# Holding four loads behind the first weight quarter, two 256-column pieces to a PSUM bank, and two later chunk pairs

## The chip, the cores and the metric

The program runs on one core of one Trainium2 chip. The metric is the device time of one execution in microseconds; the figure given for a kernel is the median of several executions. A profile is one further execution, recorded by the hardware profiler. Its span runs from the first to the last instruction of the core and is a little shorter than that execution's device time.

The engines have the profile's names: PE (matrix multiplies, with PEld for its weight loads), DVE, ACT, POOL and SP. SP issues most loads, POOL issues the weight loads and most stores, and both kinds of transfer are carried by the core's 16 DMA engines.

## The reference

A retention layer (a linear recurrence per head) feeds a low-rank mixer with a two-layer MLP.

```python
def _attn_ref(q, k, v):                      # B=4, H=8, S=768, D=64
    gamma = 1.0 - 2.0 ** (-5.0 - np.arange(H))
    for t in range(S):
        state = gamma * state + np.einsum('bhd,bhe->bhde', k[:, :, t], v[:, :, t])
        y[:, :, t] = scale * np.einsum('bhd,bhde->bhe', q[:, :, t], state)

def _moe_ref(x, U, V, w_ch1, w_ch2):         # x: 4 x 768 x 512, rank 32, hidden 2048
    xt = x.transpose(0, 2, 1)
    h = xt @ U @ V
    u = x + h.transpose(0, 2, 1)
    ch = np.maximum(u @ w_ch1, 0.0) @ w_ch2
    return u + ch
```

All inputs and the output are float32.

## The kernel before

The four batches go one after the other. The sequence of 768 positions is cut into six chunks of 128, handled as three pairs (chunks 0 and 1, 2 and 3, 4 and 5). Batch 0's attention is written out by hand as the string `STEPS` and runs first, while the weights are loaded. From there on PE's order is made by `weave` (the last lines of the body): the MLP of batch b is a list of pieces with costs in microseconds of PE time (41.472 in all for a batch), and the attention of batch b+1, with the rest of the low-rank product, is a list of marks. A mark is placed at a fraction of the list's cost, and it is emitted before the first piece that begins at or behind that fraction. Every engine executes its instructions in the order in which they are emitted.

**The MLP of a batch** (`mlp_pieces`). There are 16 hidden blocks `m` of 128 rows. `up(m, 0, 512)` makes four matmuls of 512 columns into one PSUM bank, and a relu evicts the bank to `gT`; this is done for all 16 blocks. Then `up(m, 512, 256)` does the same for the remaining 256 columns, 16 times, each with a bank and a relu of its own. Every third relu goes to DVE (L427), the others to ACT (L429). Last come 24 pieces of `down` (L445), four to each of six row blocks `j`; the fourth evicts through DVE (L452). PSUM banks with the tag `mlp` are three in number and are shared by `up`, `down` and, for batch 1, the PE transposes of k and q (`turn_k1` L257, `turn_q1` L271) and `lr_proj_turn`. A new bank waits for the eviction of what it held.

**The attention of batches 1 to 3.** For a chunk `ci`: `prep` scales or casts k, q and v (POOL or ACT, L81, L83, L77) into buffers of which there are four for each of the three; `turn_*` transposes k and q; `score` (L281) makes the scores of one chunk in the PSUM tile `R[ci % 2]` and DVE masks them (L284); `mix` writes the chunk's result over the same tile (L297, L302), ACT evicts it to `x` (L70), PE updates the state (L313), and ACT evicts the state to `nsz` in two instructions. In the table `AT`, batch 1 has the entries `(0.565, 0.095, (0.045, 0.09), (0.075, 0.045), None)`: the first pair's score stands at 0.565, each later pair's 0.095 behind it, the mixes 0.045 and 0.09 behind their score, and the transposes of k and q 0.075 and 0.045 before it. The ACT casts of k are marked at 0.51 (chunks 2 and 3) and 0.63 (chunks 4 and 5). `lr_proj_turn` stands at 0.875 and `lr_uT`, which makes the MLP's input of batch 1, at 0.915.

**The loads around the weights.** w1 comes in four quarters of 512 columns and w2 in four parts, all issued by POOL in one queue and cast on the way. Step `w0` issues w1's first quarter behind a POOL copy that waits for batch 0's last q load, and `w1` the second. The first MLP matmuls of batch 0 (`begin_up`, L400) need the first quarter. Loads of batches 1 to 3 are issued by SP in the fixed order `feed` through a ring of 20 buffers; `feed_more` issues as many as `n_open` and the ring allow. Behind `STEPS`, six loads of batch 1 are let go at once (k, q and v of chunks 0 and 1). The rest stand behind a gate: POOL copies one element of w1's column 1023 into the next ring buffer, so that the load into this buffer, and every load queued behind it on SP, waits until the second quarter has landed.

Of the kernel before, what the change touches and what calls it, by code (L numbers as in the profile page):

```python
# [16 lines left out]
def kernel(  # L17
# [11 lines left out]
    nc = tc.nc  # L29
# [98 lines left out]
    def feed_more(t=None):  # L128
        while n_fed[0] < n_open[0] and n_held[0] < RING:
            nm, b, ci = key = feed[n_fed[0]]  # L130
            n_fed[0] += 1
            n_held[0] += 1
            ready[key] = t = ring() if t is None else t
            if (nm, b) == ("q", 1):
                load_heads(t, q, 1, ci % 2, ci // 2)
            else:
                nc.sync.dma_start(
                    out=t.rearrange("p (h d) -> p h d", h=H),
                    in_=src_of[nm][b, :, ts(ci, P), :].rearrange("h p d -> p h d"))
            t = None  # L140
# [269 lines left out]
    def mlp_pieces(b):  # L410
        gT = gtp.tile([P, NM, S], bf16, tag="gT", name=f"gT_{b}")
        pieces = []
        n = [0]

        def up(m, lo, sz):
            def f():
                g_p = begun.pop((b, m, lo), None)
                c0 = 3 if g_p is not None else 0
                if not c0:
                    g_p = bank("mlp")  # L420
                for c in range(c0, NCB):
                    nc.tensor.matmul(g_p[:, :sz], w1b[:, c, ts(m, P)],  # L422
                                     uTs[b][:, c, ds(lo, sz)], start=(c == 0),
                                     stop=(c == NCB - 1))
                n[0] += 1
                if n[0] % 3 == 0:
                    nc.vector.tensor_relu(gT[:, m, ds(lo, sz)], g_p[:, :sz])  # L427
                else:
                    nc.scalar.activation(gT[:, m, ds(lo, sz)], g_p[:, :sz],  # L429
                                         AF.Relu)  # L430
            return f

        for m in range(NM):
            pieces.append((0.864, up(m, 0, LO)))
        for m in range(NM):
            pieces.append((0.432, up(m, LO, S - LO)))
        hold = {}

        def down(j, m0, n0=0, nn=DM):
            def f():  # L440
                if m0 == 0:
                    hold[j, n0] = bank("mlp")
                ch = hold[j, n0]
                for m in range(m0, m0 + 4):
                    nc.tensor.matmul(ch[:, :nn], gT[:, m, ts(j, P)],  # L445
                                     w2b[:, m, ds(n0, nn)],
                                     start=(m == 0), stop=(m == NM - 1))
                if m0 == NM - 4:
                    o_sb = outp.tile([P, DM], fp32, tag="o_sb",
                                     name=f"o_{b}_{j}_{n0}")[:, :nn]  # L450
                    n = ds(n0, nn)
                    nc.vector.tensor_tensor(o_sb, ch[:, :nn], us[b][:, j, n],  # L452
                                            op=ALU.add)
                    if n0:
                        nc.sync.dma_start(out=out[b, ts(j, P), n], in_=o_sb)
                    else:
                        stores.append((nc.gpsimd, out[b, ts(j, P), n], o_sb))
            return f

        for j in range(NCK):  # L460
            if (b, j) == (B - 1, NCK - 1):
                for n0, nn in ((0, 384), (384, 128)):
                    for m0 in range(0, NM, 4):
                        pieces.append((0.864 * nn / DM, down(j, m0, n0, nn)))
                continue
            for m0 in range(0, NM, 4):
                pieces.append((0.864, down(j, m0)))
        return pieces
# [204 lines left out]
    def step(s):  # L673
        if s[0] == "F":
            s, n = s[1:].split(":")
            return fill(s[:-1], int(s[-1]), int(n))
        if s == "Va":
            return nc.gpsimd.tensor_copy(out=V1b, in_=V1)
        if s == "Vb":
            for i, n in enumerate((512, 256)):  # L680
                nc.tensor.matmul(R[1][:, i, :n], rep4, V1b[:, ds(512 * i, n)],
                                 start=True, stop=True)
            return
        if s == "Vc":
            return evac("D", V4, R[1].rearrange("p i n -> p (i n)")[:, :S])
        nm, at = s.rstrip("0123456789."), s.lstrip("KQVWTkqSmsMNxtPpcERUbuwB")
        u = int(at[0]) if at else 0
        eng = BY[nm][u] if nm in BY and nm != "pc" else None
        if nm in ("K", "Q", "V"):
            if eng == "S":  # L690
                cast_unit("v", u, "P", 0, 2)
            else:
                cast_unit(nm.lower(), u, eng)
        elif nm == "W":
            cast_unit("v", u, "D", 2, 2)
        elif nm in ("Tk", "Tq"):
            turn_unit(nm[1], u)
        elif nm in ("kT", "qT"):
            turned_unit(nm[0], u, eng)
        elif nm == "S":  # L700
            score_unit(u)
        elif nm == "m":
            mask_unit(u)
        elif nm == "ST":
            state_unit(u, int(at[2]))
        elif nm == "s":
            state_out(u, int(at[2]), eng)
        elif nm == "M":
            mix_unit(u)
        elif nm == "N":  # L710
            query_unit(u, False)
        elif nm == "x":
            x_out(u, eng)
        elif nm == "Ub":
            evac("A", Ub, Uf)
        elif nm == "xt":
            x_turn(u)
        elif nm == "P":
            proj(u, range(NCK if u == 0 else 4))
        elif nm == "R":  # L720
            proj(1, range(4, NCK))
        elif nm == "pc":
            pc_out(u // 2, BY["pc"][u // 2])
        elif nm == "E":
            expand((0, 1) if u == 0 else (u,))
        elif nm == "B":
            for m in range(2):
                begin_up(m, (0, 1) if u == 1 else (2,))
        elif nm == "u":
            evac(eng, uTs[0][:, u, :LO], xT[u][:, :LO])  # L730
        elif nm == "w":
            if u == 0:
                nc.gpsimd.tensor_copy(out=gate0, in_=ready["q", 5][:1, :1])
            load_w1(512 * u, 512)
        else:
            raise ValueError(s)
# [9 lines left out]
    pieces0 = mlp_pieces(0)  # L746
    for s in STEPS.split():
        step(s)
    n_open[0] = 6
    feed_more()  # L750
    n_open[0] = 6 * NCK
    for mb in range(2, 4):
        load_w1(512 * mb, 512)
    for j in range(4):
        load_w2(j)
    gate = ring()
    nc.gpsimd.tensor_copy(out=gate[:1, :1], in_=w1b[:1, NCB - 1, 1023:1024])
    feed_more(gate)
    for t in nsz:
        nc.gpsimd.memset(t, 0.0)  # L760
    for nm in "kqv":
# [1 line left out]

    AT = {1: (0.565, 0.095, (0.045, 0.09), (0.075, 0.045), None),
          2: (0.255, 0.17, (0.05, 0.095), (0.175, 0.11),
              (0.0, 0.085, 0.17, 0.255, 0.34, 0.425)),
          3: (0.20, 0.20, (0.05, 0.095), (0.19, 0.145),
# [11 lines left out]
    for b in range(1, B):  # L781
        s0, step, dm, dt, at_prep = AT[b]
        for ci in range(NCK):
            pair_at = b - 1 + s0 + step * (ci // 2)
            if b == 1:
                mark(pair_at - dt[0], turn_k1, ci)
                mark(pair_at - dt[1], turn_q1, ci)
            else:
                mark(b - 1 + at_prep[ci], prep_chunk, b, ci)
                mark(pair_at - dt[ci % 2], turn_chunk, b, ci)  # L790
            mark(pair_at, score, b, ci)
            mark(pair_at + dm[ci % 2], mix, b, ci)
            if b > 2:
                mark(b - 2 + 0.25 + 0.1 * ci, open_chunk)
        if b == 1:
            for nm, eng, at in (("k", "A", (0.51, 0.63)), ("q", "P", (0.54, 0.66)),
                                ("v", "P", (0.58, 0.70))):
                for pp in (1, 2):
                    mark(at[pp - 1], prep_two, nm, pp, eng)
            mark(0.875, lr_open, b)  # L800
            mark(0.875, lr_proj_turn, b)
            mark(0.915, lr_uT, b)
            mark(1.11, lr_expand, b, 0, 4)
        else:
            l0, l1, l2, l3 = LR
            mark(b - 1 + l0, mixed, b)
            mark(b - 1 + l1, lr_expand, b, 0, 4)
            mark(b - 1 + l2, lr_turn, b, 0)
            mark(b - 1 + l3, lr_turn, b, 2)
        mark(b + 0.02, lr_expand, b, 4, 2)  # L810
        mark(b + 0.08, lr_turn, b, 4)
# [35 lines left out]
```

## Time and profile before

| What | Value |
|---|---|
| Device time, 3 runs | 228.85, 228.23 and 228.86 us; median 228.85 us |
| Device time of the profiled execution | 227.64 us |
| Its span, first to last instruction | 225.8 us |
| Granted PE clock in the span | 1.000 |
| DVE busy | 98.7 us (44%) |
| ACT busy | 86.7 us (38%) |
| POOL busy | 78.5 us (35%) |
| HBM read, written | 27.46 MB, 6.29 MB |

Busy time is the union of an engine's recorded instructions. Matmuls overlap and their ends are modelled, so a short wait of PE shows in the distance between starts before it shows as idle time. A row of the timeline gives the start, the length, the engine, the line, the tiles (out<-in), the shapes and how many equal instructions were merged; in square brackets stands the idle time before it and what ended it.

### The profile page before, as it was taken

Reading aid. Unit: us, or ns where it says so; the run is one execution under the profiler, and the core shown is the slowest. Engines: PE = TensorE matmul, PEld = TensorE weight load, DVE = VectorE, ACT = ScalarE, POOL = GpSimd, SP = SyncE. Lnnn points to the kernel's source line nnn. Section 1 sums busy time; section 2 is a strip of 40 time slices with the busy share of each in tenths; the row PEclk is TensorE's granted clock in tenths of the full one; section 3 lists DMA queues with packets and bytes.
Section 4 is the critical chain, followed back from the end, with each engine's and each line's share of the span. In section 5 each row is a group of like instructions: output and inputs, shape, how many; then the busy total and the mean of one; then the engine's idle time right before and its main releaser. Section 6 shows DMA issues by size and latency. Waiting matters only on the chain.

```text
span 225.8 us, 4802 instructions
## 1 busy us (share of the span) xinstructions
PE 216.5 (96%) x1982; PEld 122.8 (54%) x1982; DVE 98.7 (44%) x148; ACT 86.7 (38%) x180; POOL 78.5 (35%) x112
## 2 busy tenths in 40 slices
PE   7999899999899999999999999999999999999991
PEld 2567344875565544588454444686554444764451
DVE  6578536346734346625426145361624242312111
ACT  3776354554653134575230044746030044530000
POOL 5588581108720069380100496710101100001010
PEclk9999999999999999999999999999999999999999
DMA  5999999999999995889994554411113330001211
GB/s 164 336 290 249 219 198 197 196 244 221 281 253 238 247 276 98 187 186 187 206 269 133 163 139 90 99 26 25 46 49 120 115 93 0 0 3 48 93 77 64
DMA packets 89303, 34.59 MB, mean 153 GB/s; under 512 B 71217, under 2 KB 87729, under 8 KB 89281
## 3 DMA queue, kind: packets, MB, share of 16 engines
q1 hardware_dynamic: 83152, 23.86, 47.4%
q0 software_dynamic: 6128, 10.42, 18.2%
q8 instruction: 15, 0.25, 0.4%
q14 instruction: 8, 0.06, 0.1%
HBM read 27.46 MB, written 6.29 MB: 149 GB/s over the span
## 4 chain that ended last, share of the span: by engine, by line
PE 49%; issue 32%; DMA 5%; SPq 5%; POOL 4%; ACT 1%; DVE 1%; POOLq 0%
PE mlp L422 23%; PE mlp L445 18%; SPq L106 5%; DMA w1b<-in_moe_w_ch_dram 3%; POOL out_dram L408 3%; DMA in<-in_q_dram 2%; PE r L281 1%; PE r L302 1%; POOL vd L83 1%; PE r L297 1%; PE st L313 1%; PE r L344 1%; PE mlp L400 1%; DVE a L284 1%; PE mlp L271 1%
## 5 line engine op out<-in xcount | busy, mean ns | idle before, releaser
L445 PE MATMUL mlp<-w2b,gT 128*128 128x512 bf16 (+2 forms) x400 | 87.8, 371 | 0.0
L422 PE MATMUL mlp<-uT,w1b 128*128 128x512 bf16 (+1 forms) x506 | 86.4, 325 | 0.5 <-ACT gT L429 0.4
L429 ACT ACTIVATE gT<-mlp 128x512 bf16<-128x512 f32 (+1 forms) x88 | 42.3, 490 | 70.5 <-PE mlp L422 69.5
L422 PEld LDWEIGHTS <-w1b 128*128 128x128 bf16 x506 | 48.3, 98 | 32.5 <-issue 1.4
L445 PEld LDWEIGHTS <-gT 128*128 128x128 bf16 x400 | 37.0, 98 | 39.2 <-issue 0.2
L408 POOL DMA_DIRECT2D out_dram<-o x24 | 13.3, 553 | 109.1 <-DVE o L452 105.7
L427 DVE TENSOR_SCALAR gT<-mlp 128x512 bf16<-128x512 f32 (+1 forms) x40 | 22.1, 556 | 41.3 <-PE mlp L422 41.2
L452 DVE TENSOR_TENSOR o<-mlp,u 128x512 f32<-128x512 f32 (+2 forms) x25 | 16.7, 670 | 51.0 <-PE mlp L445 50.8
L284 DVE TENSOR_TENSOR a<-r,mask 128x1024 bf16<-128x1024 f32 x18 | 21.3, 1219 | 5.2 <-PE r L281 3.8
L83 POOL TENSOR_TENSOR vd<-in,gk 128x512 bf16<-128x512 f32 x18 | 18.6, 1040 | 10.0 <-PE mlp L422 5.7
L70 ACT ACTIVATE x<-r 128x512 bf16<-128x512 f32 x20 | 11.9, 596 | 25.1 <-PE r L302 24.0
L351 DVE TENSOR_TENSOR u<-r,x 128x512 bf16<-128x512 f32 (+1 forms) x16 | 14.5, 950 | 4.2 <-PE r L344 4.2
L83 POOL TENSOR_TENSOR qd<-in,gq 128x512 bf16<-128x512 f32 x12 | 12.5, 1039 | 0.0
L70 ACT ACTIVATE nsz<-st 64x256 bf16<-64x256 f32 x30 | 11.1, 372 | 0.3
L81 POOL CAST kd<-in 128x512 bf16<-128x512 f32 x14 | 8.5, 608 | 6.8 <-issue 6.2
L83 POOL TENSOR_TENSOR qp<-in,gq 128x512 bf16<-128x512 f32 x6 | 6.1, 1040 | 7.5 <-DMA in<-in_q_dram 6.0
L578 DVE TENSOR_TENSOR a<-r,mask 128x1024 bf16<-128x1024 f32 x6 | 7.3, 1220 | 2.1 <-PE r L571 2.1
L302 PE MATMUL r<-vd,a 128*128 128x64 bf16 x144 | 7.1, 193 | 0.0
L281 PE MATMUL r<-qT,kT 64*128 64x128 bf16 x144 | 5.8, 217 | 0.9 <-ACT x L70 0.9
L302 PEld LDWEIGHTS <-a 128*128 128x128 bf16 x144 | 6.0, 98 | 0.7
L281 PEld LDWEIGHTS <-kT 64*128 64x128 bf16 x144 | 4.1, 94 | 4.1 <-issue 4.0
L297 PEld LDWEIGHTS <-qT 128*128 128x128 bf16 x60 | 4.6, 98 | 2.7
(108 smaller groups left out, 143.2 us busy)
## 6 DMA issues: line engine op xcount, KB each, us to landing
in<-in_k_dram SPq DMA_DIRECT2D x24, 256.0 KB, 4.7
in<-in_q_dram SPq DMA_DIRECT2D x24, 256.0 KB, 4.8
in<-in_v_dram SPq DMA_DIRECT2D x24, 256.0 KB, 5.0
out_dram<-o POOLq DMA_DIRECT2D x23, 256.0 KB, 2.4
w1b<-in_moe_w_ch_dram POOLq DMA_DIRECT2D x4, 512.0 KB, 10.5
w2b<-in_moe_w_ch_dram POOLq DMA_DIRECT2D x4, 512.0 KB, 20.5
kT<-kd SPq DMA_TRANSPOSE x12, 2.4
qT<-qd SPq DMA_TRANSPOSE x12, 2.4
```

Source lines behind the costliest of these rows:

```text
L70: nc.scalar.activation(dst, src, AF.Copy)
L83: e.tensor_tensor(dst, src, scale, op=ALU.mult)
L281: nc.tensor.matmul(r[:, i, ts(hp, P)], kT[ri, hp], qT[ri, hp], start=True, stop=True)
L284: nc.vector.tensor_tensor(a, r.rearrange("p i (n m) -> p i n m", n=4), mask[:, None, None, :].to_broadcast([P, 2, 4, P]), op=ALU.mult)
L302: nc.tensor.matmul(o[:, ts(h, D)], a[:, i, hp], vb[:, h], start=(ci == 0 and h == 0), stop=True, skip_group_check=True)
L351: nc.vector.tensor_tensor(v4(us[b][:, ds(j0, nj), e]), R[g][:, :, :nj * P].rearrange("p c (j e) -> p c j e", j=nj), v4(xs[b][:, ds(j0, nj) ...
L408: eng.dma_start(out=dst, in_=src)
L422: nc.tensor.matmul(g_p[:, :sz], w1b[:, c, ts(m, P)], uTs[b][:, c, ds(lo, sz)], start=(c == 0), stop=(c == NCB - 1))
L427: nc.vector.tensor_relu(gT[:, m, ds(lo, sz)], g_p[:, :sz])
L429: nc.scalar.activation(gT[:, m, ds(lo, sz)], g_p[:, :sz], AF.Relu)
L445: nc.tensor.matmul(ch[:, :nn], gT[:, m, ts(j, P)], w2b[:, m, ds(n0, nn)], start=(m == 0), stop=(m == NM - 1))
L452: nc.vector.tensor_tensor(o_sb, ch[:, :nn], us[b][:, j, n], op=ALU.add)
```

## The change

Three things change.

1. The six loads are split. The two k loads go at once; the four loads of q and v stand behind a new gate on w1's column 511 (the last of its first quarter). On POOL, the third quarter of w1 is issued before this gate, the fourth quarter and w2 behind it. The gate on column 1023 stays for the rest of the loads.
2. The 16 pieces of 256 columns become eight pieces of two blocks. Each writes both halves of one bank with eight matmuls, and one relu evicts both. `relu` is now a helper that still gives every third eviction to DVE, so a batch has 24 instead of 32 relus.
3. Batch 1's score marks become 0.565, 0.685 and 0.80 (before: 0.565, 0.66 and 0.755). The mixes and transposes of k and q move with their pair; the casts of `prep_two` stay. `lr_open` and `lr_proj_turn` move from 0.875 to 0.905 and `lr_uT` from 0.915 to 0.94.

```diff
+        def relu(dst, src):
+            n[0] += 1
+            if n[0] % 3 == 0:
+                nc.vector.tensor_relu(dst, src)
+            else:
+                nc.scalar.activation(dst, src, AF.Relu)
+
...
-        for m in range(NM):
-            pieces.append((0.432, up(m, LO, S - LO)))
+        def up_two(m):
+            def f():
+                g_p = bank("mlp")
+                for n in range(2):
+                    for c in range(NCB):
+                        nc.tensor.matmul(g_p[:, ts(n, S - LO)], w1b[:, c, ts(m + n, P)],
+                                         uTs[b][:, c, LO:], start=(c == 0),
+                                         stop=(c == NCB - 1))
+                relu(gT[:, ds(m, 2), LO:], g_p.rearrange("p (n t) -> p n t", n=2))
+            return f
+
+        for m in range(0, NM, 2):
+            pieces.append((0.864, up_two(m)))
...
+    def feed_behind(col):
+        gate = ring()
+        nc.gpsimd.tensor_copy(out=gate[:1, :1], in_=w1b[:1, NCB - 1, col:col + 1])
+        feed_more(gate)
+
+    n_open[0] = 2
+    feed_more()
+    load_w1(1024, 512)
     n_open[0] = 6
-    feed_more()
+    feed_behind(511)
     n_open[0] = 6 * NCK
-    for mb in range(2, 4):
-        load_w1(512 * mb, 512)
+    load_w1(1536, 512)
     for j in range(4):
         load_w2(j)
-    gate = ring()
-    nc.gpsimd.tensor_copy(out=gate[:1, :1], in_=w1b[:1, NCB - 1, 1023:1024])
-    feed_more(gate)
+    feed_behind(1023)
...
-    AT = {1: (0.565, 0.095, (0.045, 0.09), (0.075, 0.045), None),
+    AT = {1: ((0.565, 0.685, 0.80), None, (0.045, 0.09), (0.075, 0.045), None),
...
-            pair_at = b - 1 + s0 + step * (ci // 2)
+            pair_at = b - 1 + (s0[ci // 2] if b == 1 else s0 + step * (ci // 2))
...
-            mark(0.875, lr_open, b)
-            mark(0.875, lr_proj_turn, b)
-            mark(0.915, lr_uT, b)
+            mark(0.905, lr_open, b)
+            mark(0.905, lr_proj_turn, b)
+            mark(0.94, lr_uT, b)
```

More of the change, by code (lines that the diff above doesn't have):

```diff
@@ L424, in f @@
                                      stop=(c == NCB - 1))
[L425 to L430, printed above, removed]
+                relu(gT[:, m, ds(lo, sz)], g_p[:, :sz])
             return f
```

## The prediction

> **What bounds the kernel now.** The first view is the page's head, the second PE's waits (microseconds in total, times, longest).
>
> ```profile
> span 225.8 us, 4802 instructions
> PE 216.5 (96%) x1982; PEld 122.8 (54%) x1982; DVE 98.7 (44%) x148; ACT 86.7 (38%) x180; POOL 78.5 (35%) x112
> ```
> ```profile
> PE r L281 <- ACT x L70: 0.9, 1, 0.9
> PE mlp L400 <- DMA w1b<-in_moe_w_ch_dram: 0.7, 1, 0.7
> PE mlp L422 <- ACT gT L429: 0.4, 2, 0.2
> ```
>
> PE sets the end. No matmul is removed, so only PE's waits can be won, and three are named here: a score behind ACT, the first MLP matmul behind w1, `up` behind relus. The third is larger than it looks, since matmul ends are modelled; the timeline's starts tell it. First batch 3 without attention (60 matmuls of 512 columns and 64 of 256 in one row), then the 256-column stage of batch 1, then that of batch 2.
>
> ```profile
> 180.31 20.11 PE L422 MATMUL mlp<-uT,w1b 128*128 128x512 bf16 x124
> 200.26 20.92 PE L445 MATMUL mlp<-w2b,gT 128*128 128x512 bf16 x112
> ```
> ```profile
> 97.71 1.47 PE L422 MATMUL mlp<-uT,w1b 128*128 128x256 bf16 x12
> 99.41 1.91 PE L422 MATMUL mlp<-uT,w1b 128*128 128x256 bf16 x16 [0.23 <-ACT gT L429]
> 101.25 0.62 PE L281 MATMUL r<-qT,kT 64*128 64x128 bf16 x16
> 101.80 2.55 PE L422 MATMUL mlp<-uT,w1b 128*128 128x256 bf16 x20
> 104.19 0.39 PE L297 MATMUL r<-nsz,qT 128*128 128x128 bf16 x4
> ...
> 104.87 1.04 PE L422 MATMUL mlp<-uT,w1b 128*128 128x256 bf16 x8
> 105.74 1.03 PE L445 MATMUL mlp<-w2b,gT 128*128 128x512 bf16 x4
> ```
> ```profile
> 145.01 4.25 PE L422 MATMUL mlp<-uT,w1b 128*128 128x512 bf16 x32
> ...
> 155.62 2.75 PE L445 MATMUL mlp<-w2b,gT 128*128 128x512 bf16 x12
> ```
>
> Batch 3: 60 matmuls of 512 columns and 64 of 256 take 19.95, so 0.217 and 0.1084 each: the price without waits. Batch 1, 97.71 to 105.74: 8.03, less 56 x 0.1084 = 6.07, the score (0.55) and the mix (104.19 to 104.87, 0.68), leaves 0.73. Batch 2, 145.01 to 155.62: 10.61, less 4 x 0.217, 64 x 0.1084, 0.55 and 2 x 0.68, leaves 0.89. About 0.1 each is PE's switch into a score (0.31 between starts instead of 0.217, also where nothing waits). Waits: 0.63 + 0.79 = 1.42.
>
> **The w1 quarter.** Transfers on the two queues (packets, MB, share of 16 engines) from 21 to 23 us:
>
> ```profile
> q0 software_dynamic: 374, 0.38, 118.0%
> q1 hardware_dynamic: 36, 0.01, 2.5%
> ```
> From 23 to 24 us:
> ```profile
> q1 hardware_dynamic: 389, 0.20, 69.2%
> q0 software_dynamic: 76, 0.07, 52.7%
> ```
> From 27 to 47 us:
> ```profile
> q0 software_dynamic: 3105, 3.08, 90.6%
> q1 hardware_dynamic: 3102, 0.84, 30.3%
> ```
>
> q0 is the weights', with 1 KB a packet, so a quarter is 512. Alone it moves 187 a us; from 23 the batch 1 loads share, and it moves 76. By 23 it has moved 84 (20 to 21) + 374; the 54 left end near 23.8 now, near 23.3 alone. The quarter lands at 25.48 (17.99 + 7.49 in the chain) and PE starts at 25.52. I move the landing 0.5 to 0.7 earlier; PE is ready at 24.83, DVE's casts of uT follow until 26.14 and cap it. Gain 0.6 (bounds 0 and 0.70, the whole wait).
>
> What is moved: POOL's gate holds w1's last quarter and w2's four issues, before at 22.0 to 25.8, to about 24.9 to 28.9. Quarters two and three stay queued (landed 29.1 and 32.6, some 7 us of work), so q0 does not run dry, at no cost. Behind the gate on POOL also stand the second gate, the memsets of `nsz` and the casts of chunks 0 and 1, which PE first wants at 47.55. On SP the four loads, and all behind them, start some 6.5 later than 17.9. They are 2 x 512 packets (512 B) and 2 x 1,024 (256 B); with the weights they go one for one, 155 a us each (3,105 in 20 us), and alone 785 (5,101 in 49.5 to 56). The next, k of chunk 3, is the one that PE comes to wait for: it landed at about 50.5, where ACT's cast of it began; qT behind the cast ended at 51.78, the score came at 52.18. Before this k stand the same weight and load packets as now, and the DMA row of the page shows 9 in every slice from 6 to 84 us, so it still lands near 50.5. The score is wanted 0.3 earlier (0.6 here less 0.28 below) with 0.4 of cover; I take 0.1 of loss (bounds 0 and 0.4). Every us beyond costs one. v's two POOL casts are wanted by the mixes at 54.9 and 58.1, and at a landing of 44.2 + 6.5 they are still in time.
>
> **Two pieces to a bank.** ACT's relu is 0.38 for 256 columns and 0.60 for 512, DVE's 0.42 and 0.69. What makes PE wait is ACT's queue: an `x` (0.60) and two `nsz` (0.77) stand before a relu, while the three banks cover 3 x 0.432 = 1.30 of PE. With 3 x 0.864 = 2.59 they cover it, as in the 512-column pieces with the same marks (92.55 to 97), where PE keeps its pace. I walked the built order of batches 1 and 2 with these durations: the least room is 0.3, behind DVE's two masks (2.4). Gain 1.42 (bounds: a loss of 0.22 ACT or 0.27 DVE at each of the two named waits, 0.5, and 1.42). One loss is certain: batch 0's first `down` takes the bank of the last relu, now eviction 24 on DVE. It waited until 48.18 behind 0.41 on ACT from 47.72; 0.69 makes it 0.28 later.
>
> The Trainium skill, "Perfetto Trace Analysis", section "Optimizing Scalar/DVE Operations", speaks against this edit: engines that are not saturated but cause bubbles elsewhere should get smaller instructions. ACT at 38% and DVE at 44% are such engines. By the rule the two named waits grow by 0.5 in all instead of 1.42 going, and the total is +0.4, about 229.2. I go by the rows, as the bank rotation doubles with the instruction.
>
> **The later pairs.** ACT and PE around the long wait:
>
> ```profile
> 58.28 0.39 PE L313 MATMUL st<-vd,kd 128*128 128x128 bf16 x4
> ...
> 58.76 0.63 ACT L77 ACTIVATE kd<-in 128x512 bf16<-128x512 f32 x1 [0.91 <-issue]
> ...
> 59.29 0.58 ACT L70 ACTIVATE x<-r 128x512 bf16<-128x512 f32 x1
> ```
>
> The k cast of chunk 5 needs chunk 1's buffer, which its state matmuls free at 58.67; `x` of chunk 1 stands behind the cast, and the score of chunk 3 behind `x`: 1.08 lost. Before it, a q transpose waits 0.29 for a bank (55.37 to 55.88). The set-back puts four down matmuls (0.87) between mix and score. But the cast stays at 0.63, and in the built order the eviction of qT of chunk 2 (0.74) now stands behind it, and kT of chunk 2 (0.60) behind `x` and `nsz` of chunk 0. Counted from chunk 0's mix V: `nsz` ends at V+1.70, kT at V+2.32, so the q transpose, ready at V+1.80, waits 0.57. Chunk 1's state ends near V+4.5; cast, qT and `x` end at V+5.24, 5.88 and 6.32; the two scores, ready at V+5.31 and 6.13, wait 0.6 and 0.25. That is 1.44 for 1.37: cost 0.07 (bounds: all 1.37 won, 0.6 lost if the next bank waits too). `lr_uT` loses two `down` pieces of cover: DVE's eviction of R[1] (1.21) ends 1.66 after its matmuls start, PE has 2.1 of work: 0.
>
> **Sum.** -0.60 (w1) - 1.42 (relus) + 0.28 (last eviction) + 0.07 (pairs) + 0.05 (uT's cast) + 0.10 (k of chunk 3) = -1.52. Span 225.8 to 224.3; the profiled execution 227.64 to 226.1. The median of the runs is 1.2 above that execution: 228.85 - 1.52 = 227.3.
>
> **Rivals.**
> - The set-back works in full: the pairs' 1.44 goes too, 227.3 - 1.44 = 225.9. For: the score's wait is the largest named. Against: the order on ACT.
> - The waits only move: relus hold banks 0.2 longer and the quarter is late (0.2 won), so -0.2 + 0.5 + 0.28 + 0.07 = +0.65 at worst, and with half of the bank gain -0.2 - 0.7 + 0.35 = -0.55; the middle is 228.9. For: only 0.3 of room behind the masks.
> - Slower: the held loads are late for chunk 3's k cast. If the 6.5 of later start came through in full, k would land at 57.0; at half, 53.75, which is 3.25 past 50.5: 227.2 (the sum without the 0.1) + 3.25 = 230.4. It decides from a landing near 52.1 on, where it has eaten the 1.6. For: the longest of these loads took 22.2 from issue to landing. Against: the same packets stand before it.
>
> **Chances.** Forecast 0.62 (its own range 226.6 to 228.1), full set-back 0.13, waits only move 0.15, late loads 0.10. A measurement tells about 0.3% (0.7 us) from no change. Faster: 0.58 + 0.13 = 0.71; same 0.04 + 0.13 = 0.17; slower 0.02 + 0.10 = 0.12. The range 226.0 to 229.0 takes in the second rival's middle and most of the way to the first, and leaves the slower one out.
>
> **What would show it.** L400 starting near 24.9 without a w1 wait; no `up` wait in batches 1 and 2, and the stretch that went from 145.01 to 155.62 shorter by 0.8; batch 0's first `down` 0.91 behind the k transposes' start; a q transpose and two scores of the second pair waiting for ACT, 1.4 in all. Wrong if ACT's k cast of chunk 3 starts past 51, or if PE's waits there are under 0.5.

## The result and the profile after

| | Before | After |
|---|---|---|
| Median of 18 runs each | 228.86 us | 227.50 us |
| Lowest to highest | 227.97 to 231.39 us | 225.75 to 229.67 us |
| Profiled execution | 227.64 us | 227.32 us |
| Its span | 225.8 us | 225.5 us |

The ratio after to before is 0.9925, 95% interval 0.9896 to 0.9953: faster by 1.7 us, between 1.1 and 2.4. (Ratios, here and below, leave out executions more than 1.5% above the fastest of the same kernel, for e4 four of twelve and for e10 three of six, while medians are of all, so that a ratio is not the quotient of the medians.) The two profiled executions differ by only 0.3 us. That alone says that one execution of each is not enough here, and where they differ must be found stage by stage. First the head of the page of the changed kernel, then PE's waits in it (total us, times, longest us).

```profile
span 225.5 us, 4740 instructions
...
PE 213.9 (95%) x1955; PEld 122.6 (54%) x1982; DVE 98.6 (44%) x140; ACT 82.2 (36%) x156; POOL 78.7 (35%) x113
```
```profile
...
PE st L605 <- POOL vu L81: 1.2, 2, 1.0
PE st L605 <- POOL vu L83: 0.9, 2, 0.4
PE r L281 <- ACT qT L70: 0.5, 1, 0.5
PE mlp L271 <- ACT kT L70: 0.4, 1, 0.4
PE mlp L458 <- DVE gT L418: 0.3, 1, 0.3
```

The rows for `up` behind relus, for L400 behind w1 and for the score behind `x` are gone. New are a q transpose behind `kT`, a score behind `qT`, the first `down` behind DVE's relu, and 2.1 us of waits for POOL in batch 0's attention (L605). The code of batch 0's attention is the same in both kernels.

The timeline of PE in the changed kernel shows the three places. (Some records of matmuls are missing, so a count can be one short: the x5 of L400 stands for six.) First where batch 0's attention ends and the first MLP matmuls (L400) begin. Before:

```profile
24.44 0.39 PE L669 MATMUL r<-V,pc 32*128 32x512 bf16 x1
25.52 1.47 PE L400 MATMUL mlp<-uT,w1b 128*128 128x512 bf16 x6 [0.70 <-DMA w1b<-in_moe_w_ch_dram]
```

In the changed kernel, with DVE's second cast of `uT`:

```profile
25.80 0.39 PE L682 MATMUL r<-V,pc 32*128 32x512 bf16 x1
26.12 1.47 PE L400 MATMUL mlp<-uT,w1b 128*128 128x512 bf16 x5
26.82 0.68 DVE L72 CAST uT<-r 128x512 bf16<-128x512 f32 x1
27.56 0.59 PE L429 MATMUL mlp<-uT,w1b 128*128 128x512 bf16 x2
```

Here PE did not wait for w1, whose quarter had landed only just before, at 26.08. The last expand came at 25.80 instead of 24.44, because batch 0's last v loads landed 1.5 us later in this execution, and with it L400 is 0.6 late. The next matmuls (L429) begin where the cast of `uT` ends, 1.43 behind L400; before they began 1.31 behind it.

Next, the 256-column stage of batch 2:

```profile
145.50 0.81 PE L429 MATMUL mlp<-uT,w1b 128*128 128x512 bf16 x3
146.37 3.66 PE L442 MATMUL mlp<-uT,w1b 128*128 128x256 bf16 x32
149.96 0.62 PE L281 MATMUL r<-qT,kT 64*128 64x128 bf16 x16
150.51 1.92 PE L442 MATMUL mlp<-uT,w1b 128*128 128x256 bf16 x16
...
152.95 1.91 PE L442 MATMUL mlp<-uT,w1b 128*128 128x256 bf16 x16
...
155.37 1.89 PE L458 MATMUL mlp<-w2b,gT 128*128 128x512 bf16 x7
```

The 32 matmuls take 3.59 up to the start of the score, 0.1 of it PE's switch, so 0.109 each: the pace of batch 3. From 145.50 to 155.37 are 9.87 us; the same work took 10.61 before (145.01 to 155.62).

Last, ACT and PE in the second pair of batch 1:

```profile
57.22 0.60 ACT L70 ACTIVATE kT<-mlp 128x512 bf16<-128x512 f32 x1
57.71 0.62 ACT L77 ACTIVATE kd<-in 128x512 bf16<-128x512 f32 x1
57.87 0.61 PE L271 MATMUL mlp<-ident,qp 128*128 128x128 bf16 x8 [0.44 <-ACT kT L70]
...
60.10 0.63 ACT L77 ACTIVATE kd<-in 128x512 bf16<-128x512 f32 x1 [1.77 <-PE st L313]
60.64 0.73 ACT L70 ACTIVATE qT<-mlp 128x512 bf16<-128x512 f32 x1
61.23 0.58 ACT L70 ACTIVATE x<-r 128x512 bf16<-128x512 f32 x1
61.42 0.84 PE L281 MATMUL r<-qT,kT 64*128 64x128 bf16 x16 [0.54 <-ACT qT L70]
```

The k cast of chunk 5 sits on ACT until PE's state of chunk 1 frees its buffer (idle for 1.77 us), with `qT` and `x` behind it, and the scores wait for these. Between starts PE loses 0.60 at the q transpose, 0.70 at the first score and 0.20 at the second.

Since the start differs from execution to execution, the table counts from L400. "First `down`" and "first score" belong to the MLP of batch 0 and batch 1's chunk 0. "Stage 1" is the stretch from batch 1's first expand (L344) to batch 2's projection (L335), "stage 2" that from batch 2's first expand to batch 3's projection; each holds one 256-column stage.

| Kernel profiled | L400 at | L400 to first down | to first score | to batch 1's expand | Stage 1 | Stage 2 | L400 to end |
|---|---|---|---|---|---|---|---|
| before | 25.52 | 22.66 | 26.66 | 55.45 | 36.84 | 47.77 | 200.33 |
| after | 26.12 | 23.10 | 27.09 | 55.92 | 36.26 | 47.04 | 199.43 |

From L400 on the change wins 0.90.

### The profile page after: what moved, and what is told of

Read it like the earlier page. It is cut to its first block, busy times and chain, and to the rows that moved or that the text cites. A ratio compares the mean times of both kernels' runs of the same rounds, so it can differ in the third digit from the quotient of the medians.

```text
span 225.5 us, 4740 instructions
## 1 busy us (share of the span) xinstructions
PE 213.9 (95%) x1955; PEld 122.6 (54%) x1982; DVE 98.6 (44%) x140; ACT 82.2 (36%) x156; POOL 78.7 (35%) x113
## 4 chain that ended last, share of the span: by engine, by line
PE 52%; issue 31%; SPq 6%; POOL 4%; DMA 2%; ACT 1%; DVE 0%; POOLq 0%; ACTq 0%
PE mlp L458 18%; PE mlp L429 17%; PE mlp L442 6%; SPq L106 5%; POOL out_dram L408 3%; DMA in<-in_v_dram 2%; PE r L281 2%; PE r L302 1%; PE st L313 1%; PE r L297 1%; POOL vd L83 1%; PE r L344 1%; PE mlp L271 1%; PE mlp L400 1%; POOL qd L83 0%
## 5 line engine op out<-in xcount | busy, mean ns | idle before, releaser
L458 PE MATMUL mlp<-w2b,gT 128*128 128x512 bf16 (+2 forms) x384 | 86.2, 370 | 1.3 <-DVE gT L418 0.3
L420 ACT ACTIVATE gT<-mlp 128x512 bf16<-128x512 f32 x64 | 38.1, 597 | 70.0 <-PE mlp L429 57.1
L429 PE MATMUL mlp<-uT,w1b 128*128 128x512 bf16 x243 | 56.1, 379 | 0.3
L418 DVE TENSOR_SCALAR gT<-mlp 128x512 bf16<-128x512 f32 x32 | 22.1, 690 | 45.4 <-PE mlp L429 23.9
L429 PEld LDWEIGHTS <-w1b 128*128 128x128 bf16 x250 | 23.6, 98 | 27.4 <-issue 0.2
L442 PE MATMUL mlp<-uT,w1b 128*128 128x256 bf16 x256 | 29.4, 273 | 0.1
```

The source lines that it names most:

```text
L418: nc.vector.tensor_relu(dst, src)
L420: nc.scalar.activation(dst, src, AF.Relu)
L429: nc.tensor.matmul(g_p[:, :sz], w1b[:, c, ts(m, P)], uTs[b][:, c, ds(lo, sz)], start=(c == 0), stop=(c == NCB - 1))
L442: nc.tensor.matmul(g_p[:, ts(n, S - LO)], w1b[:, c, ts(m + n, P)], uTs[b][:, c, LO:], start=(c == 0), stop=(c == NCB - 1))
L458: nc.tensor.matmul(ch[:, :nn], gT[:, m, ts(j, P)], w2b[:, m, ds(n0, nn)], start=(m == 0), stop=(m == NM - 1))
```

## The experiments

All kernels were timed in turn with the kernel before on the same chip. Readings by stage come from one profiled execution each.

**The change again, and its three parts alone.** The parts are the blocks of the diff shown above, put alone into the kernel before.

```diff
 a0_again: the changed kernel
 e1_two_to_a_bank: only
-        for m in range(NM):
-            pieces.append((0.432, up(m, LO, S - LO)))
+        for m in range(0, NM, 2):
+            pieces.append((0.864, up_two(m)))
 e2_hold: only
+    n_open[0] = 2
+    feed_more()
+    load_w1(1024, 512)
+    n_open[0] = 6
+    feed_behind(511)
 e3_pairs: only
-    AT = {1: (0.565, 0.095, (0.045, 0.09), (0.075, 0.045), None),
+    AT = {1: ((0.565, 0.685, 0.80), None, (0.045, 0.09), (0.075, 0.045), None),
```

Expected of the change again:

> The changed kernel once more, as the measure for its three parts on the same chip. My sum: -1.52 (226.0 to 229.0 against a before of 228.85). In its trace, from the low-rank expand of batch 0 to the end of the span, 1.5 to 1.7 less than in the kernel before; the start ahead of this expand may differ by a microsecond either way from execution to execution, if it is the loads' landing and not the change that moved it in the first profile.

Of the bank pairs alone:

> The kernel before with only the 256-column pieces two to a bank. My theory: the waits of these stages in batches 1 and 2 go (-1.42) and the first down of batch 0 waits 0.28 longer: -1.1 (the stretch from batch 1's last state to its first down 0.6 shorter, batch 2's 0.8). Rival (longer relus only hold banks longer, as a rule for smaller instructions has it): +0.3 to +0.8, with up waits left in both stages.

Of the held loads alone:

> The kernel before with only the four loads held. My theory: L400 starts 0.6 to 0.7 earlier against the expand ahead of it, without a wait for w1; the k cast of chunk 3 starts within 0.5 of 50.5 and hides all beyond its 0.4 of cover, so -0.3 to -0.6. Rival (held loads are late one for one, or half): k of chunk 3 lands at 53.7 or later and the sum is +2.5 or more. Second rival (the loads did not slow w1): the wait for w1 stays, 0.0.

Of the set-back pairs alone:

> The kernel before with only batch 1's later pairs and its low-rank marks set back. My theory: the score's wait of 0.9 is exchanged for a q transpose waiting 0.5 and two scores waiting 0.5 and 0.2, as the cast of k and x stand ahead on ACT: 0.0 to +0.2. Rival (the set-back works in full): -1.4, with no PE wait over 0.2 for ACT in the second pair.

| Kernel | Median us (before: 228.55) | Ratio, 95% interval | L400 at | to first down | to first score | to batch 1's expand | Stage 1 | Stage 2 | L400 to end |
|---|---|---|---|---|---|---|---|---|---|
| a0_again | 227.82 | 0.9946 (0.9917 to 0.9975) | 26.88 | 22.97 | 26.97 | 55.79 | 36.26 | 47.04 | 199.26 |
| e1_two_to_a_bank | 227.55 | 0.9943 (0.9899 to 0.9987) | 26.14 | 23.07 | 27.06 | 55.86 | 36.26 | 47.04 | 199.34 |
| e2_hold | 228.16 | 0.9964 (0.9935 to 0.9993) | 26.92 | 24.24 | 28.24 | 57.04 | 36.84 | 47.77 | 201.87 |
| e3_pairs | 228.49 | 0.9974 (0.9938 to 1.0010) | 25.84 | 22.66 | 26.66 | 55.49 | 36.84 | 47.77 | 200.36 |

The stages repeat to a few hundredths, so they tell the parts apart where the medians, with intervals of 0.6 us and more to either side, do not.

*Bank pairs.* Stage 1 is 0.58 shorter and stage 2 0.73, the first `down` 0.41 later; together with the end, L400 to the end is 0.99 shorter. PE's waits in this kernel have no `up` row any more, the score's wait of 0.9 is still there, and the new one is the first `down`:

```profile
PE r L281 <- ACT x L70: 0.9, 1, 0.9
...
PE mlp L458 <- DVE gT L418: 0.3, 1, 0.3
```

The rival, that longer relus only hold the banks longer, is out: the `up` waits are gone in both batches. Two things changed at once, though: a bank covers twice the work of PE, and two blocks are evicted in 0.60 instead of 0.76 on ACT. No run changes one without the other; that the cover decides is argued from ACT's queue and not shown by itself.

*Set-back pairs.* L400 to the end changes by +0.03, the waits as expected: where the score waited 0.9 for `x`, PE's waits now have

```profile
PE r L281 <- ACT qT L70: 0.5, 1, 0.5
PE mlp L271 <- ACT kT L70: 0.4, 1, 0.4
```

The rival of a full gain (-1.4) is out.

*Held loads.* The second rival fits: k of chunk 3 was in time, but the wait for w1 is there, 1.3 us before L400, and so it is in the changed kernel run again. (The ratio of e2 alone, 0.2 to 1.5 us faster, would leave room for the gain; e5 and e9 below, without the hold, don't bear it out.) PE's first wait there, and then the transfers of the two queues from 23 to 25 us in the same execution:

```profile
PE mlp L400 <- DMA w1b<-in_moe_w_ch_dram: 1.4, 1, 1.4
```
```profile
q0 software_dynamic: 275, 0.27, 101.5%
```

There is no row of the load queue, so nothing shares, and still the weights moved 275 packets in 2 us, 137 a us, where I had reckoned with 187 alone. The quarter landed at 26.83, 8.46 behind its issue; unheld it had taken 7.48 (before), 8.03 (e1) and 7.66 (e3), held 7.80 (after), 8.46 and 8.49 (e2). (In the profile of e2 the granted clock was 0.65 from 28 to 32 us, which is why its columns up to batch 1's expand are long.) So the hold does not bring the quarter in earlier. The trace also holds 16 packets of 4 bytes for each weight load. Of the first 16 in a0_again, which I take to be those of w1's first quarter, 12 are through at 24.32 and the last at 26.50; before, 12 at 23.43 and the last at 25.15. The Trainium skill, "DMA: Bandwidth & Descriptors", section "Why a DMA increments its semaphore by 16 and not by 1", says what such a packet can be: each of 16 DMA engines adds one to the semaphore when its own share is in, they finish independently, and only the full 16 means that all has landed. The trace agrees: the quarter counts as landed some 0.3 us behind the last of the 16. So what PE waits for is the slowest share, in these two profiles some two us behind the twelfth, and a mean rate says nothing of it. Which engine is late, and why, the trace does not tell.

**Holding more, holding nothing, and the order on ACT.** The next four kernels start from the changed one.

```diff
 e4_hold_six (k of chunks 0 and 1 held too)
-    n_open[0] = 2
-    feed_more()
 e5_no_hold (the loads and gates of the kernel before)
+    n_open[0] = 6
+    feed_more()
+    n_open[0] = 6 * NCK
+    for mb in range(2, 4):
+        load_w1(512 * mb, 512)
 e6_k_order
-                mark(pair_at - dt[0], turn_k1, ci)
+                mark(0.59 if ci in (2, 3) else pair_at - dt[0], turn_k1, ci)
...
-            for nm, eng, at in (("k", "A", (0.51, 0.63)), ("q", "P", (0.54, 0.66)),
+            for nm, eng, at in (("k", "A", (0.51, 0.69)), ("q", "P", (0.54, 0.66)),
 e7_k_order_first: e6 and
-                mark(0.59 if ci in (2, 3) else pair_at - dt[0], turn_k1, ci)
+                mark({0: 0.475, 2: 0.59, 3: 0.59}.get(ci, pair_at - dt[0]), turn_k1, ci)
```

Expected of the six held loads:

> The changed kernel with all six loads, k of chunks 0 and 1 too, held behind w1's first quarter, so that behind batch 0's own loads nothing shares the DMA engines with it. Theory A (the first profiles): the quarter is in when the slowest of its 16 shares is in, 7.5 to 8.5 after its issue, and the held loads don't set it; L400 starts at the same time on the median (26.2, span less what follows L400), and the time is that of the changed kernel within 0.4. Theory B (my prediction's step: the sharing costs 0.6): the quarter lands under 7.3 after its issue and L400 has no wait for it. Theory C (late loads cost): k of chunk 3 lands 0.5 or more later than 51.15 and the score of chunk 0 waits for ACT; slower by 0.3 to 1.

Of no hold:

> The changed kernel with the loads and gates of the kernel before (bank pairs and set-back pairs stay). Theory A (the hold wins nothing): the same as the changed kernel within 0.3, -1.0 against before, and the same -0.9 to -1.1 from L400 to the end. Theory B (the hold wins 0.6 of the wait for w1): 0.6 slower than the changed kernel, -0.7 or less against before.

Of the two moved marks:

> The changed kernel with two marks of batch 1 moved: the k transposes of chunks 2 and 3 ahead of the mix of chunk 0 (0.59 instead of 0.61), and ACT's k casts of chunks 4 and 5 behind the scores of chunks 2 and 3 (0.69 instead of 0.63). My theory (the set-back pairs wait because of the order on ACT: kT behind x and nsz, qT and x behind the cast): the q transpose and the scores of chunks 2 and 3 wait for nothing, L400 to the end 1.2 to 1.4 shorter than in the changed kernel (198.0 to 198.2 after 199.3 to 199.4), -2.3 against before. Rival (the waits only move, to the k transposes of chunks 4 and 5 behind the later casts, or to DVE's masks): 0.6 or less of it.

Of the earlier first k transpose:

> As the kernel with the two marks moved, and batch 1's first k transpose set ahead of batch 0's last piece of up (0.475 instead of 0.49), so that its first down finds a bank whose eviction is done. My theory (the first down waits for DVE's last relu and nothing else): the wait of 0.4 to 0.5 ahead of the first down goes, L400 to the first down 22.6 instead of 23.0 to 23.1, and the sum -2.7 against before. Rival (the wait goes to the second k transpose or the last up, which now wait for the relus ahead of them): 0.2 or less.

| Kernel | Median us (before: 228.83) | Ratio, 95% interval | L400 at | to first down | to first score | to batch 1's expand | L400 to end |
|---|---|---|---|---|---|---|---|
| e4_hold_six | 229.04 | 0.9990 (0.9953 to 1.0027) | 26.02 | 23.33 | 31.82 | 61.96 | 205.43 |
| e5_no_hold | 227.16 | 0.9945 (0.9913 to 0.9978) | 26.41 | 23.28 | 27.28 | 56.11 | 199.59 |
| e6_k_order | 226.02 | 0.9898 (0.9855 to 0.9940) | 25.93 | 22.97 | 26.96 | 54.38 | 197.86 |
| e7_k_order_first | 225.45 | 0.9888 (0.9842 to 0.9934) | 24.85 | 22.58 | 26.79 | 54.20 | 197.70 |

*Six held.* Here the late load that I had as the slower rival is to be seen. ACT's two k casts and the first score in the timeline:

```profile
53.86 0.63 ACT L77 ACTIVATE kd<-in 128x512 bf16<-128x512 f32 x1 [4.37 <-POOL vd L83]
56.53 0.63 ACT L77 ACTIVATE kd<-in 128x512 bf16<-128x512 f32 x1 [2.05 <-DMA in<-in_k_dram]
57.07 0.72 ACT L70 ACTIVATE qT<-mlp 128x512 bf16<-128x512 f32 x1
57.84 1.04 PE L281 MATMUL r<-qT,kT 64*128 64x128 bf16 x16 [3.45 <-ACT qT L70]
```

k of chunk 3 landed at 56.51 instead of 51.15, ACT waited for it, and `qT` and the score behind it. The wait is 3.45 us. The stretch from L400 to the first score grew by 4.7, in it also 0.81 of a q transpose that waited for POOL's scaling of q, which was late too. Behind the wait the granted clock fell, to 0.55 from 58 to 61, and the stretch from the score to batch 1's expand grew by another 1.3. Not every execution has it: this one is the slowest of twelve (233.23 us), and among those at full clock the span runs from 224.6 to 227.9. By the ratios (0.9990 here, 0.9945 for e5) the kernel loses some 1.0 us against the changed one, with intervals that overlap. The quarter landed 5.74 behind its issue in this profile, all 16 shares by 24.14, sooner than in any other kernel, and L400, with no wait for it, was still not earlier (26.02), as PE was not ready before. So theory B holds for the quarter here, in one execution, and theory C for the time: what the start may win is less than what the late k costs.

*No hold.* The time is that of the changed kernel within the intervals (0.9945 and 0.9946). From L400 on the unheld kernel takes 0.16 to 0.33 longer: between the two expands of batch 0 at L344 it takes 6.14 instead of 5.95, while w1's second quarter lands at 30.46 instead of 28.61. (Against a0_again 0.14 more is the cast of `uT`, which shows where L400 did not wait for w1.) Over all profiles the hold does bring the second quarter in sooner: it lands 2.5 to 2.8 us behind the first with the four loads held (3.55 in e2), and 3.6 to 4.1 without. But PE has work to cover most of this: the five unheld profiles take 5.96 to 6.14 between the two expands, where the changed kernel takes 5.95.

To see the hold's worth at the start over more than one profile: every execution has a span, and with the stretch from L400 to the end of its kernel's profile taken off (for e2 that of the kernel before), what is left is where L400 began. Over all executions at a granted clock of 0.998 or more, of all kernels but e4, this gives:

| | Executions | Mean | Median | Lowest, highest |
|---|---|---|---|---|
| with the hold (after, a0, e2, e6, e7, e8, e10) | 38 | 26.23 | 26.16 | 24.5, 27.7 |
| without it (before, e1, e3, e5, e9) | 42 | 26.23 | 26.17 | 24.4, 27.7 |

The means differ by 0.0, with 0.3 to either side as the 95% interval (resampled, all executions taken alike). By kernel they go from 26.0 to 26.7 with the hold and from 25.7 to 26.4 without. A step of 0.6 in the hold's favour is excluded. (The last three kernels follow below.)

The 13 profiles also tell what an earlier quarter could win at most. Where PE itself is ready last, L400 starts 0.32 behind the last expand (e4, e5); in `after`, e7 and e9 it lost 0.05 or less to w1. So in five of them there was nothing to win, and in the other eight the wait was 0.2 to 1.4. From issue to landing the quarter took 7.39 to 8.91 us with four loads held and 6.90 to 8.03 without.

*Order on ACT.* L400 to the end is 1.4 to 1.6 shorter than in the changed kernel (197.86 after 199.26 and 199.43; 198.0 to 198.2 was expected), and the median follows. The same place in the timeline:

```profile
56.07 0.60 ACT L70 ACTIVATE x<-r 128x512 bf16<-128x512 f32 x1 [0.66 <-PE r L302]
...
56.95 0.61 PE L271 MATMUL mlp<-ident,qp 128*128 128x128 bf16 x8
57.38 0.74 ACT L70 ACTIVATE qT<-mlp 128x512 bf16<-128x512 f32 x1
...
59.90 0.62 PE L281 MATMUL r<-qT,kT 64*128 64x128 bf16 x16
60.20 1.15 ACT L77 ACTIVATE kd<-in 128x512 bf16<-128x512 f32 x2
```

Neither the q transposes nor the scores wait; the casts (0.63 each) run behind the scores, still ahead of the next k transposes.

*Earlier first k transpose.* The first `down` comes 0.39 sooner, but only 0.17 of it reaches the first score (counted from batch 0's first expand, ahead of which e7 has 0.09 of `uT`'s cast, 0.48 and 0.26): the second q transpose now waits 0.22 for a bank, behind DVE's `kT`, which stands behind the last relu. Both theories had a part of it.

```profile
47.39 0.69 DVE L418 TENSOR_SCALAR gT<-mlp 128x512 bf16<-128x512 f32 x1 [2.15 <-PE mlp L442]
47.43 1.02 PE L458 MATMUL mlp<-w2b,gT 128*128 128x512 bf16 x3
48.00 0.68 DVE L72 CAST kT<-mlp 128x512 bf16<-128x512 f32 x1
48.29 0.83 PE L271 MATMUL mlp<-ident,qp 128*128 128x128 bf16 x8
```

**Three last kernels**, from e7.

```diff
 e8_q_later
-                mark(pair_at - dt[1], turn_q1, ci)
+                mark(0.54 if ci < 2 else pair_at - dt[1], turn_q1, ci)
 e9_no_hold_best: e8 with the loads and gates of the kernel before
 e10_w1_sooner: e8 and
-                nc.gpsimd.tensor_copy(out=gate0, in_=ready["q", 5][:1, :1])
+                nc.gpsimd.tensor_copy(out=gate0, in_=ready["k", 5][:1, :1])
```

Expected of the later q transposes:

> The kernel with the k order and the earlier first k transpose, and batch 1's first q transposes one piece of down later (0.54 instead of 0.52), where the run before showed the second of them waiting 0.22 for DVE's kT. Expected: L400 to the first score's end 0.2 shorter, L400 to the end 197.5 (197.7 before), -2.7 against before. Rival (ACT's qT, later by a piece, holds the first score): 0.0 or a loss up to 0.5.

Of the same without the hold:

> The same kernel with the loads and gates of the kernel before. Theory A (the hold wins nothing for the start; it spares only some tenths of waiting for w1's second quarter): within 0.3 of the kernel with the hold. Theory B (the hold wins 0.6): 0.6 slower than it.

Of the sooner w1:

> The kernel with the hold and the later q transposes, and w1's first quarter issued behind POOL's wait for k of unit 5 instead of q of unit 5, 0.2 to 0.9 sooner. Theory A (the quarter lands 7.4 to 8.5 after its issue whatever shares, so L400 follows the issue): issue at 17.2 to 17.5, landing near 25, the wait for w1 ahead of L400 under 0.5, and 0.2 to 0.5 faster than without it. Rival (the weights now take packets from batch 0's last v loads, one for one, and batch 0's states wait for these): 0.0 or slower by up to 0.5.

| Kernel | Median us (before: 229.12) | Ratio, 95% interval | L400 at | to first down | to first score | to batch 1's expand | L400 to end |
|---|---|---|---|---|---|---|---|
| e8_q_later | 226.36 | 0.9871 (0.9821 to 0.9921) | 26.84 | 22.49 | 26.48 | 53.89 | 197.64 |
| e9_no_hold_best | 224.96 | 0.9830 (0.9785 to 0.9875) | 25.27 | 22.65 | 26.64 | 54.05 | 197.61 |
| e10_w1_sooner | 227.00 | 0.9836 (0.9777 to 0.9895) | 25.75 | 22.49 | 26.48 | 53.89 | 197.37 |

The later q transposes win 0.31 up to the first score; 0.09 of it is `uT`'s cast, which e8, waiting for w1, does not show, so 0.22, as expected. (L400 to the end is longer in e8 than in e10 from batch 1's expand on, at granted clocks of 0.998 and 0.999; the code behind it is the same.) Without the hold the kernel is no slower, which is theory A again; of the 0.16 that e9 is later at the first `down`, 0.08 lies between the two expands at L344, the other 0.08 is `uT`'s cast. The last kernel did not test its theory: k of unit 5 landed only 0.76 ahead of q, POOL's cast of it took the time, and w1 was issued at 17.85, not sooner than in e8 (17.89). Its quarter landed 7.85 later, within the spread of all others.

The lowest median is that of e9, though the intervals do not set it apart from e7, e8 and e10: two pieces to a bank, the pairs set back together with the k casts and k transposes that stood in their way, and no hold. From L400 on it is 2.7 us shorter than the kernel before; the measured gain, 1.25 to 2.15%, has besides an early start: in its six executions 25.1 to 26.0 lies ahead of L400.

## Why the prediction was right, and where it was not

The forecast was 227.3 us and the median 227.5, but one of its two large terms is not there, so that it came this close is in part luck.

- **The w1 quarter (-0.60): wrong.** The failed step is "the 54 left end near 23.8 now, near 23.3 alone", from which I took a "Gain 0.6". Alone the queue did not keep 187 packets a us in those microseconds (137 in a0_again), and the landing hangs on the slowest of 16 shares. Over 38 and 42 executions the hold changed the start of L400 by 0.0, 0.3 to either side. The sharing that I reckoned with is there for the second quarter, which lands 1 us or more sooner behind the first with the hold; PE's work covers all of this but 0 to 0.2. That the profile of before showed a wait of 0.70 and a start at 25.52 was one draw from a spread of three us. Why the slowest share of the first quarter is late stays open. The held loads themselves started 8.5 later than before (26.34 after 17.86), not 6.5.
- **Two pieces to a bank (-1.42): right.** Measured alone: -0.58 (0.63 was the term) and -0.73 (0.79), and the least room behind the masks was enough. The Trainium skill's advice to break instructions up, which I had put against it ("Perfetto Trace Analysis", section "Optimizing Scalar/DVE Operations"; the page says only that this may help), did not fit here: with the larger relu the `up` waits went, as the bank doubles along with it. Still smaller relus were not tried.
- **The last eviction (+0.28): right, a little small.** The first `down` comes 0.95 behind the k transposes' start (0.91 was the sum), 0.63 before. To L400 it is 0.31 (a0_again) to 0.44 (`after`) later; the difference is `uT`'s cast.
- **The later pairs (+0.07): right.** A q transpose and two scores wait 0.60, 0.70 and 0.20 (0.57, 0.6 and 0.25), and alone the part costs 0.03. That the cause is the order on ACT, e6 shows: two marks moved, and 1.4 to 1.6 us are won.
- **uT's cast (+0.05): there when w1 is not late.** The prediction gives no working for the 0.05. It is 0.13 in the profile after (L429 starts 1.43 behind L400, right behind the cast, instead of 1.31) and 0 in a0_again, where PE waited for w1.
- **k of chunk 3 (+0.10): not seen.** From the first `down` to batch 1's expand the changed kernel takes 32.82, before 32.79, which leaves 0.03 for the pairs and this. The k cast of chunk 3 started at 51.17, past the 51 that I had named, but L400 was itself 0.6 late; counted from L400 it is 25.05 against 25.00 before, and 0.77 lay between the end of `qT` (52.44) and the score (53.21).

From L400 on my terms sum to -0.92; measured are -0.90 and -1.07. At the start I had -0.60 and it is 0. So the traces give -1.0, and the comparisons -1.7 (1.1 to 2.4) and -1.2 (0.6 to 1.9). The second contains -1.0, the first just does not; what may be left of it has no place in the traces. The forecast has 0.6 that is not there, and the comparison some tenths that no trace shows: that these two make up for each other is luck, and not the mechanism.

The rivals: the full set-back fell with e3, and holds once the ACT order is changed (e6). "The waits only move" fell with e1. The late loads did not occur, but e4 shows that they are real: with two more loads held, k of chunk 3 landed at 56.51 in one execution (57.0 was the price in full), and the lower clock came on top.

## What to carry to other kernels

When an engine stalls for evictions, ask how much work a buffer of the rotation covers, not how long the eviction is: twice the piece for 1.6 times the eviction won a microsecond. Setting work back helps only if the instruction that it really waits for is not fixed ahead of it in the evicting engine's order; move that one too. Before pricing a load that shares the DMA engines by its rate, see how the same landing varies over executions: here one profile showed a wait of 0.7 us, the next ones 0 to 0.9 with the same loads, and 0 to 1.4 with the hold that was to end it.

## What the hardware showed that was not expected

- The start of L400, behind the loads of batch 0, varied from 24.4 to 27.7 us over 80 executions, more than the whole change brings, while what follows repeated to 0.2 us in the two profiles of the changed kernel (199.43 and 199.26).
- The sixteenth of the 4-byte packets behind w1's first quarter, a transfer of 512 packets, came 0.7 to 2.3 us behind the twelfth in twelve of the 13 profiles, and 0.3 in e4.
- A wait of 3.45 us was followed by three us at a granted clock of 0.55, with `down` matmuls 0.31 to 0.43 apart instead of 0.217. In e2 a wait of 1.3 us was followed by 0.65 from 28 to 32 us, and in a0_again one of 1.4 us by a clock that stayed at 1.00.
